# Three stages on one core: the first MoE's order written out by hand, and the second gate taken by 32-column blocks

## The chip, the cores and the metric

The kernel runs on one core of a Trainium2 chip. The metric is the device time of one execution in microseconds; 1963.57 is the median of three runs of the kernel before, which gave 1962.87 to 1965.89. TensorE is called PE, VectorE DVE, ScalarE ACT, GpSimd POOL, and SyncE, which issues most transfers, SP.

## The reference

Linear attention over 4 x 768 tokens gives x of 3072 tokens by 384. A first mixture of experts sends each token to one of 8 experts; a second one uses all 8 and weights them by a matrix P that is normalised by rows and columns in turn:

```python
# first MoE, top 1
e_idx = np.argmax(x @ w_gate, axis=1)
for e in range(E):
    mask = e_idx == e
    h = np.maximum(x[mask] @ w1[e], 0.0)
    out[mask] = gate_w[mask, None] * eom[mask, e, None] * (h @ w2[e])
...
# second MoE, all experts
logits = x @ w_gate
P = np.exp(logits - logits.max())
for _ in range(8):
    P /= P.sum(1, keepdims=True) + 1e-09
    P /= P.sum(0, keepdims=True) + 1e-09
    P *= N / E
for e in range(E):
    out += P[:, e:e + 1] * (np.maximum(x @ w1[e], 0.0) @ w2[e])
```

The arithmetic is float32. The kernel gets it from fp32r matmuls by splitting each operand into a high part (a cast) and a low part (the difference), with three matmuls for a product: high by high, high by low, low by high.

## The kernel before, in words

**Stage A** (0 to some 180 us) is the attention and the first gate. It leaves the tokens sorted by expert in device memory (`xs`), and 24 scatters on POOL (`tokd`, L785) still run when stage B begins.

**Stage B**, the first MoE, is a loop over 64 units `u` (8 experts by 8 slices of 128 hidden columns). `m_load` (L925) brings an expert's tokens in four transfers of 104 x 384 into one buffer `xe`, `m_tr` (L935) turns them with 12 PE transposes and splits them into `xh` and `xl`. A unit has nine matmuls of the first layer (`m_l1`, L958, into one of two PSUM buffers `l`), a split ReLU (`split_relu`: ACT L806 writes `hhm`, DVE L807 `hlm`), and, two units later, nine matmuls of the second layer (`m_l2`, L971). The weights of a unit come in one transfer on SP into one of three buffers `raw` (`w_load`, L99) and are split into `slot` by ACT (L112) and DVE (L113) in `w_conv`, six units ahead of their use at the start. At the end of an expert its three results are copied into `x2` (L976).

Work for stage C is put between the units in the program: `w_sums(0)` (sums of the second MoE's weights, POOL L832 to L837, from the transfers `ra` L817 and `rb` L822), `w_split(0, 0..2)` (their splits `wah` on ACT L850 and `wal` on DVE L851), called at units 58 to 60, and by the table `EARLY` sums of blocks of `x2` (`x_sum`, L890 and L891, on the engine that the table names, G for POOL, V for DVE) and their splits (`x_split`, ACT L900, DVE L901). Stage B is written in this order, but a scheduler may move each instruction within its engine's queue; each engine then runs its queue strictly in order. A branch (`If`, L1011) follows for tokens that overflow; it isn't taken here.

**Stage C**, the second MoE, has 32 units, each of 15 "products" of three fp32r matmuls with 512 columns (`product`, L1129) into the PSUM banks S, T, Z and W in the order of the table `ORDER`; `reads` adds or copies a bank into `hc` (ACT L1139, DVE L1142 to L1148) before the next product may use that bank. From unit 2 on the second layer's matmuls (`triple`, L1176) stand between the products. Here PE, DVE and ACT keep the order of the program (`manual_schedule`); POOL and SP are still the scheduler's. In unit 0 the remaining sums and splits of `x2` follow the table `FIRST`.

The second gate (`p_logits`, L1070) has for each of 24 token blocks of 128 three matmuls: the tokens are the stationary operand, the 8 gate columns (`wg2_raw`) move. Three are issued after each product of unit 0, four after those of unit 1. Each float32 matmul shows as two records in the trace. `p_max0` to `p_max2` (L1076 to L1090) take the maximum over all logits, subtract it and take the exponential into `pw`, in unit 1 at steps 7, 9 and 11. `sinkhorn` works on `pw` from unit 2 on.

Of the kernel before, what the change touches and what calls it, by code (L numbers as in the profile page):

```python
# [66 lines left out]
XBUF = [{"p11": 0, "p6": 1, "p3": 2, "p0": 2, "p5": 2, "p10": 2, "p1": 3, "p2": 4},  # L67
# [7 lines left out]
def linattn_moe_moe2_kernel(ctx: ExitStack, tc: tile.TileContext, a, out):  # L75
# [44 lines left out]
    maskb = const.tile([P, P], BF16, name="maskb")  # L120
# [29 lines left out]
    wg2_raw = const.tile([P, KD, E], F32, name="wg2_raw")  # L150
    nc.scalar.dma_start(wg2_raw, wg2)
# [745 lines left out]
    def x_split(hb, p):  # L897
# [7 lines left out]
             54: [("p5", V), "p9"], 55: ["p5"], 58: [("p10", V)], 62: ["p10"], 63: ["p6"], 64: ["p14"]}  # L905
# [13 lines left out]
    with ExitStack() as mctx:  # L919
# [57 lines left out]

        m_load(0)
        m_load(1)
        m_tr(0)  # L980
        NU = E * NF
        for u in range(NU + 2):
            if u < NU:
                if u + NWR < G5 + 5:
                    w_load(u + NWR)
                if u + NWR - 3 < G5 + 5:
                    w_conv(u + NWR - 3)
                if u + 2 >= G5 + 5:
                    w_conv(u + 2)
                if u + 5 >= G5 + 5:  # L990
                    w_load(u + 5)
                m_l1(u)
                if u == NU - 8:
                    r1_load(0)
                    r2_load(0)
                    w_sums(0)
                if u in (NU - 6, NU - 5, NU - 4):
                    w_split(0, u - NU + 6)
                if u == NU - 3:
                    r1_load(1)  # L1000
                if u % NF == 3:
                    m_load(u // NF + 2)
                if u % NF == 5:
                    m_tr(u // NF + 1)
            if u >= 2:
                m_l2(u - 2)
            for what in EARLY.get(u, ()):
                x_do(0, what)
# [65 lines left out]
    def p_max0():
        mxs["mx"] = m2.tile([P, 1], F32, name="pmx")
        V.tensor_reduce(mxs["mx"], mxs["lp"], AX.XY, ALU.max)  # L1076

    def p_max1():
        mp = qps.tile([P, P], F32, name="mxp", tag="o1")
        nc.tensor.transpose(mp[:1, :], mxs["mx"], ident)  # L1080
        mxs["m1"] = m2.tile([1, 1], F32, name="pm1")
# [165 lines left out]
    with tc.manual_schedule(engines={ENG.PE, ENG.DVE, ENG.Activation}):  # L1247
        for u in range(NU2):
# [4 lines left out]
            for s in range(15):  # L1253
# [99 lines left out]
```

## Time and profile before

| | |
|---|---|
| median of three runs | 1963.57 us (1962.87 to 1965.89) |
| the profiled execution, own time | 1965.2 us |
| its span, first to last instruction | 1963.4 us |
| mean granted clock of PE over the span | 0.971 |
| PE busy | 1901.3 us, 97% of the span |
| DVE, ACT, POOL busy | 1369.9, 832.9, 495.9 us (70%, 42%, 25%) |
| DMA | 123.49 MB, mean 63 GB/s |

The span is 1.8 us shorter than the time of the same execution: what lies before its first and after its last instruction. In the page's forty slices of 49 us PE is at nine tenths or more in all but five; the fifth (196 to 245 us), with the start of stage B, is at six. The granted clock is given as a share of full speed: 1.0 is 2.4 GHz, 0.5 is 1.2 GHz. A matmul's duration includes its way through the array, so what a row of several matmuls takes is the time from its start to the next row's start, not the sum of its records.

### The profile page before, as it was taken

The page shows a single profiled execution, that of the slowest core. Times are in us where ns is not written, and L with a number is a line of the kernel's source. Part 1 is how long each engine was busy: PE and PEld are TensorE (multiplying, and loading weights), DVE is VectorE, ACT ScalarE, POOL GpSimd, SP SyncE. Part 2 cuts the span into 40 slices and gives each one's busy share as a digit, 9 for nine tenths or more (in the row PEclk, how much of TensorE's full clock was granted, in tenths as well). Part 3 has the DMA queues.
Part 4 walks back from the last instruction along what each step waited for, and adds up shares of the span by engine and source line. Part 5 has one row for each costly group of instructions (what it writes and reads, how often), then busy time and mean ns, then how long its engine had stood idle before and what let it go on. Part 6 is the DMA issues. An engine that isn't in the chain of part 4 may idle for free.

```text
span 1963.4 us, 27510 instructions
## 1 busy us (share of the span) xinstructions
PE 1901.3 (97%) x10599; PEld 1723.3 (88%) x10600; DVE 1369.9 (70%) x2309; ACT 832.9 (42%) x1685; POOL 495.9 (25%) x528
## 2 busy tenths in 40 slices
PE   8988699999999999999999999999999999999998
PEld 6775699997889999999999988999999999999997
DVE  8995355564797767777667778667776777776774
ACT  4563344441545443444444344543444343434442
POOL 6786400112111121111111224311112211111112
PEclk8897899996999999999999999999999999999999
DMA  9864644210111111111111111111111111111101
GB/s 309 250 197 112 115 139 138 73 58 25 34 40 33 33 33 33 41 33 33 41 33 33 33 33 55 59 32 41 41 33 33 33 34 40 33 38 36 33 25 49
DMA packets 43987, 123.49 MB, mean 63 GB/s; under 512 B 6680, under 2 KB 10136, under 8 KB 43848
## 3 DMA queue, kind: packets, MB, share of 16 engines
q1 hardware_dynamic: 39256, 111.95, 19.5%
q0 software_dynamic: 3904, 9.47, 1.3%
q8 instruction: 85, 1.39, 0.3%
q14 instruction: 54, 0.44, 0.1%
q10 hardware_dynamic: 688, 0.23, 0.1%
HBM read 107.07 MB, written 14.56 MB: 62 GB/s over the span
## 4 chain that ended last, share of the span: by engine, by line
PE 74%; DVE 2%; issue 1%; POOL 0%; ACT 0%; POOLq 0%; DVEq 0%; ACTq 0%
PE o L1176 39%; PE bS L1129 13%; PE bT L1129 11%; PE bZ L1129 5%; PE bW L1129 4%; PE lgp L1070 1%; DVE wal L851 1%; DVE hc L1142 0%; DVE slot L901 0%; POOL out L1196 0%; DVE x L1194 0%; DVE hl L1163 0%; DVE third L901 0%; DVE xsb L890 0%; ACT slot L900 0%
## 5 line engine op out<-in xcount | busy, mean ns | idle before, releaser
L1176 PE MATMUL o<-wbh,hl 128*128 128x384 f32 x1536 | 515.1, 335 | 0.8 <-DVE hl L1163 0.7
L1176 PE MATMUL o<-wbh,hh 128*128 128x384 f32 x1536 | 514.2, 335 | 0.7 <-DVE x L1188 0.3
L1176 PE MATMUL o<-wbl,hh 128*128 128x384 f32 x1536 | 514.3, 335 | 0.0
L1163 DVE SCALAR_TENSOR_TENSOR hl<-hc,hh 128x512 fp32r<-128x512 f32 x384 | 275.2, 719 | 205.5 <-ACT hh L1162 201.6
L832 POOL TENSOR_TENSOR ws<-ra 128x384 f32<-128x384 f32 x64 | 64.9, 1014 | 1106.6 <-DVE wal L851 1023.7
L1176 PEld LDWEIGHTS o<-wbh,hh 128*128 128x128 f32 x1536 | 288.5, 188 | 46.7 <-DVE x L1194 1.1
L1176 PEld LDWEIGHTS o<-wbh,hl 128*128 128x128 f32 x1536 | 288.4, 188 | 42.4 <-DVE hl L1163 1.9
L1176 PEld LDWEIGHTS o<-wbl,hh 128*128 128x128 f32 x1536 | 288.5, 188 | 0.0
L1139 ACT COPY hc<-bT 128x512 f32<-128x512 f32 x192 | 112.7, 587 | 408.8 <-PE bT L1129 407.0
L1139 ACT COPY hc<-bS 128x512 f32<-128x512 f32 x192 | 112.5, 586 | 377.9 <-PE bS L1129 377.8
L1162 ACT ACTIVATE hh<-hc 128x512 fp32r<-128x512 f32 x384 | 240.2, 634 | 11.7 <-PE o L1176 10.3
L1129 PE MATMUL bS<-slot,wah 128*128 128x512 f32 x704 | 230.8, 402 | 8.7 <-DVE hc L1142 6.8
L1194 DVE SCALAR_TENSOR_TENSOR x<-o,pw,x 128x384 f32<-128x384 f32 x348 | 205.0, 611 | 22.4 <-PE o L1176 17.9
L1129 PE MATMUL bT<-slot,wah 128*128 128x512 f32 x640 | 205.0, 402 | 0.0
L1142 DVE TENSOR_TENSOR hc<-bS,hc 128x512 f32<-128x512 f32 x192 | 132.0, 688 | 47.0 <-PE bS L1129 45.7
L1129 PE MATMUL bS<-slot,wal 128*128 128x512 f32 x384 | 152.1, 396 | 0.0
L851 DVE TENSOR_TENSOR wal<-ws,wah 128x384 fp32r<-128x384 f32 (+2 forms) x192 | 132.6, 691 | 24.3 <-ACT wah L850 24.3
L1129 PEld LDWEIGHTS bS<-slot,wah 128*128 128x128 f32 x704 | 128.2, 190 | 11.0 <-DVE hc L1142 8.0
L1142 DVE TENSOR_TENSOR hc<-bT,hc 128x512 f32<-128x512 f32 x128 | 87.9, 687 | 56.6 <-PE bT L1129 53.7
L1129 PE MATMUL bT<-slot,wal 128*128 128x512 f32 x320 | 126.5, 395 | 0.0
L850 ACT CAST wah<-ws 128x384 fp32r<-128x384 f32 (+2 forms) x192 | 117.6, 613 | 13.7 <-POOL ws L837 13.7
L1129 PEld LDWEIGHTS bT<-slot,wah 128*128 128x128 f32 x640 | 115.7, 190 | 0.2
(227 smaller groups left out, 2915.2 us busy)
## 6 DMA issues: line engine op xcount, KB each, us to landing
raw<-in_wm SPq DMA_DIRECT2D x64, 384.0 KB
ra<-in_wm SPq DMA_DIRECT2D x64, 384.0 KB
rb<-in_wm SPq DMA_DIRECT2D x64, 384.0 KB
na<-in_nat SPq DMA_DIRECT2D x25, 576.0 KB
rk<-in_rkt SPq DMA_DIRECT2D x25, 448.0 KB
xs<-zer SPq DMA_DIRECT2D x8, 624.0 KB
xe<-xs SPq DMA_DIRECT2D x32, 156.0 KB
xs<-x,posl POOLq DMA_INDIRECT x24
```

Source lines behind the costliest of these rows:

```text
L832: G(s_[:, 0:3], r[:, 1], r[:, 0], ALU.subtract)
L850: nc.scalar.copy(hi[:, q], x)
L851: nc.vector.tensor_tensor(lo[:, q], x, hi[:, q].bitcast(F32), ALU.subtract)
L1070: nc.tensor.matmul(mxs["lp"][:, t, :], x2[:, k, t * P:(t + 1) * P], wg2_raw[:, k, :], start=(k == 0), stop=(k == KD - 1), skip_group_check ...
L1129: nc.tensor.matmul(bank[bk], w_[:, at, :], x_, start=(opens == 1 and n == 0), stop=(n == 2), skip_group_check=True)
L1139: A.copy(hid(u, *copy[p]), ps)
L1142: V.tensor_tensor(h, ps, h, ALU.add)
L1162: A.activation(hh, h, AF.Relu)
L1163: V.scalar_tensor_tensor(hl, h, 0.0, hh.bitcast(F32), ALU.max, ALU.subtract)
L1176: nc.tensor.matmul(ob[j], h_[:, j * P:(j + 1) * P], w_[:, c], start=(f == 0 and m == 0), stop=(f == 3 and m == 2))
L1194: V.scalar_tensor_tensor(acc, ob[j], wt, acc, ALU.mult, ALU.add)
```

## The change

Four things change.

1. Stage B's loop stands under `manual_schedule` for PE, DVE and ACT, so that these engines keep the program's order there too. `w_sums(1)` is now called in unit 63 of stage B, not in unit 0 of stage C.
2. The second gate has the gate's columns as the stationary operand, padded with zeros to 32 (`wg2_s`), and 512 tokens move. Blocks of tokens write PSUM partitions 0 to 31, 32 to 63 and so on: 18 matmuls of 32 x 512 in groups of four (steps 0 to 2 of unit 1) and of two (steps 3 to 5), where there were 72 of 128 x 8. ACT copies the sums to `xsb4` and `xsb3`; eight transposes (`p_turn`, steps 6 and 8 of unit 1) and two copies on DVE bring them into `pw`; the maximum follows at steps 8, 10 and 12.
3. `m_load` is one transfer of 624 KB where there were four of 156 KB.
4. The sum p1 of `x2` is taken on DVE in unit 64 of stage B, not on POOL in unit 0 of stage C, and the buffers of p1 and p2 are others.

```diff
-XBUF = [{"p11": 0, "p6": 1, "p3": 2, "p0": 2, "p5": 2, "p10": 2, "p1": 3, "p2": 4},
+XBUF = [{"p11": 0, "p6": 1, "p3": 2, "p0": 2, "p5": 2, "p10": 2, "p1": 2, "p2": 3},
...
-    wg2_raw = const.tile([P, KD, E], F32, name="wg2_raw")
-    nc.scalar.dma_start(wg2_raw, wg2)
+    wg2_s = const.tile([P, KD, 4 * E], F32, name="wg2_s")
+    nc.vector.memset(wg2_s[:, :, E:], 0.0)
+    nc.scalar.dma_start(wg2_s[:, :, 0:E], wg2)
...
-             54: [("p5", V), "p9"], 55: ["p5"], 58: [("p10", V)], 62: ["p10"], 63: ["p6"], 64: ["p14"]}
+             54: [("p5", V), "p9"], 55: ["p5"], 58: [("p10", V)], 62: ["p10"], 63: ["p6"], 64: ["p14", ("p1", V)]}
...
-            for j in range(CJ):
-                nc.sync.dma_start(t[:, j, :], xs[e * NTOK + j * CP:e * NTOK + (j + 1) * CP, :])
+            nc.sync.dma_start(t, xs[e * NTOK:e * NTOK + CAP, :].rearrange("(j p) d -> p j d", p=CP))
...
+        with tc.manual_schedule(engines={ENG.PE, ENG.DVE, ENG.Activation}):
...
+                    if u == NU - 1:
+                        w_sums(1)
...
-    def p_logits(n):
-        if "lp" not in mxs:
-            mxs["lp"] = qps.tile([P, NT, E], F32, name="lgp", tag="o0")
-        for _ in range(min(n, len(lgq))):
-            t, k = lgq.pop(0)
-            nc.tensor.matmul(mxs["lp"][:, t, :], x2[:, k, t * P:(t + 1) * P], wg2_raw[:, k, :], start=(k == 0),
-                             stop=(k == KD - 1), skip_group_check=True)
+    def p_logits(r, k):
+        nb = 4 if r == 0 else NB - 4
+        if k == 0:
+            mxs["l", r] = qps.tile([P, TB], F32, name=f"lgp{r}", tag=f"o{r}")
+        for q in range(nb):
+            n = 4 * r + q
+            nc.tensor.matmul(mxs["l", r][32 * q:32 * (q + 1), :], wg2_s[:, k, :], x2[:, k, n * TB:(n + 1) * TB],
+                             start=(k == 0), stop=(k == KD - 1), skip_group_check=True)
+        if k == KD - 1:
+            A.copy(xsb[4 - r][:32 * nb], mxs["l", r][:32 * nb])
+
+    def p_turn(r):
+        nb = 4 if r == 0 else NB - 4
+        tp = qps.tile([P, TJ, nb, 4 * E], F32, name=f"lgt{r}", tag=f"o{2 + r}")
+        for j in range(TJ):
+            nc.tensor.transpose(tp[:, j].rearrange("p q e -> p (q e)"), xsb[4 - r][:32 * nb, j * P:(j + 1) * P],
+                                ident[:32 * nb, :32 * nb])
+        V.tensor_copy(pw[:, 16 * r:16 * r + 4 * nb, :].rearrange("p (q j) e -> p j q e", j=TJ), tp[:, :, :, 0:E])
...
-        V.tensor_reduce(mxs["mx"], mxs["lp"], AX.XY, ALU.max)
+        V.tensor_reduce(mxs["mx"], pw, AX.XY, ALU.max)
...
-    FIRST = {0: ["p11", ("p1", G)], 1: ["p7"], 3: ["p12"], 4: [("p2", V)], 6: ["p1"], 7: ["p2"], 9: ["p4"]}
+    FIRST = {0: ["p11"], 1: ["p7"], 3: ["p12"], 4: [("p2", V)], 6: ["p1"], 7: ["p2"], 9: ["p4"]}
+
+    GATE = {15: [lambda: p_logits(0, 0)], 16: [lambda: p_logits(0, 1)], 17: [lambda: p_logits(0, 2)],
+            18: [lambda: p_logits(1, 0)], 19: [lambda: p_logits(1, 1)], 20: [lambda: p_logits(1, 2)],
+            21: [lambda: p_turn(0)], 23: [lambda: p_turn(1), p_max0], 25: [p_max1], 27: [p_max2]}
...
-                if u == 0:
-                    p_logits(3)
-                elif u == 1:
-                    p_logits(4)
-                    if s == 7:
-                        p_max0()
-                    if s == 9:
-                        p_max1()
-                    if s == 11:
-                        p_max2()
+                for step in GATE.get(15 * u + s, ()):
+                    step()
...
                 if s == 4:
-                    w_sums(u + 1)
+                    if u > 0:
+                        w_sums(u + 1)
```

Where instructions move: ACT's queue in the first five units of stage B, before:

```order
L112 CAST slot0_63<-raw9_2997 128x768
L806 ACTIVATE hhm3_3071<-l1_3_3061 128x416
L850 CAST wah0_0_4805<-ra0_4738 128x256
L112 CAST slot1_64<-raw10_3013 128x768
L850 CAST wah0_0_4805<-ws0_4742 128x384
L850 CAST wah0_1_4841<-ws0_4742 128x512
L850 CAST wah0_1_4841<-ra0_4738 128x128
L806 ACTIVATE hhm4_3103<-l1_4_3093 128x416
```

and the same place now (the lines are those of the changed kernel, one or more further down):

```order
L112 CAST slot0_63<-raw9_2994 128x768
L807 ACTIVATE hhm3_3068<-l1_3_3058 128x416
L112 CAST slot1_64<-raw10_3010 128x768
L807 ACTIVATE hhm4_3097<-l1_4_3087 128x416
L112 CAST slot2_65<-raw11_3026 128x768
L807 ACTIVATE hhm5_3124<-l1_5_3114 128x416
```

The casts of `wah0_*`, which read `ra0` and POOL's sums `ws0`, are no longer between the ReLUs of units 3 and 5. They stand at units 58 to 60, in the place where the program calls them; DVE's `wal0_*` go with them.

PE's queue at the start of stage C, before (each matmul of the gate counted once):

```order
L1129 MATMUL bS0_0_5179<-slot5_68,wah0_0_4805 128x512 x2
L1129 MATMUL bS0_0_5179<-slot5_68,wal0_0_4806 128x512
L1070 MATMUL lgp_5185<-wg2_raw_104,x2_2945 128x8 x3
L1129 MATMUL bT0_1_5191<-slot5_68,wah0_0_4805 128x512
L1129 MATMUL bT0_1_5191<-slot6_69,wah0_0_4805 128x512
L1129 MATMUL bT0_1_5191<-slot5_68,wal0_0_4806 128x512
```

and now, from the first step of unit 1, where the gate begins:

```order
L1143 MATMUL bS1_0_5270<-slot5_68,wah1_0_5227 128x512 x2
L1143 MATMUL bS1_0_5270<-slot5_68,wal1_0_5228 128x512
L1074 MATMUL lgp0_5276<-x2_2946,wg2_s_103 32x512 x4
L1143 MATMUL bT1_1_5281<-slot5_68,wah1_0_5227 128x512
L1143 MATMUL bT1_1_5281<-slot6_69,wah1_0_5227 128x512
L1143 MATMUL bT1_1_5281<-slot5_68,wal1_0_5228 128x512
L1074 MATMUL lgp0_5276<-x2_2946,wg2_s_103 32x512 x4
```

Unit 0's products follow one another with no gate between them, and unit 1 has a group after each of its first six.

POOL's queue behind the branch, before (`xsb` with a new number each time is another buffer; `ws` are the sums for unit 2's weights):

```order
L890 TENSOR_TENSOR xsb_5168<-x_2945 128x512
L890 TENSOR_TENSOR xsb_2956<-x_2945 128x512
L891 TENSOR_TENSOR xsb_5168<-xsb_5168,x_2945 128x512
L891 TENSOR_TENSOR xsb_2956<-xsb_2956,x_2945 128x512
L890 TENSOR_TENSOR xsb_2955<-x_2945 128x512
L891 TENSOR_TENSOR xsb_2955<-xsb_2955,x_2945 128x512
L890 TENSOR_TENSOR xsb_5168<-x_2945,xsb_2956 128x512
L891 TENSOR_TENSOR xsb_5168<-xsb_5168,xsb_2955 128x512
L890 TENSOR_TENSOR xsb_5169<-x_2945 128x512
L891 TENSOR_TENSOR xsb_5169<-xsb_5169,x_2945 128x512
L832 TENSOR_TENSOR ws_5383<-ra_5310 128x384
```

and now:

```order
L891 TENSOR_TENSOR xsb_2957<-x_2946 128x512
L892 TENSOR_TENSOR xsb_2957<-xsb_2957,x_2946 128x512
L891 TENSOR_TENSOR xsb_2956<-x_2946 128x512
L892 TENSOR_TENSOR xsb_2956<-xsb_2956,x_2946 128x512
L833 TENSOR_TENSOR ws_5318<-ra_5255 128x384
L834 TENSOR_TENSOR ws_5318<-ra_5255 128x512
L836 TENSOR_TENSOR ws_5318<-ra_5255 128x256
L837 TENSOR_TENSOR ws_5318<-ws_5318,ra_5255 128x128
L838 TENSOR_TENSOR ws_5318<-ws_5318,ra_5255 128x256
L891 TENSOR_TENSOR xsb_5159<-x_2946 128x512
L892 TENSOR_TENSOR xsb_5159<-xsb_5159,x_2946 128x512
L891 TENSOR_TENSOR xsb_5158<-x_2946,xsb_2957 128x512
```

Four of the ten sums stay at the branch. The last four, of which three show here and which write the buffers that now also hold the gate's sums, come after the sums of unit 2's weights and wait for `p_turn`. The five sums of unit 1's weights stand ahead of the branch, in POOL's queue after the sums of unit 50.

## Rows read from the trace of the kernel before

**Rows 1.** Windows: length, busy (instructions) of PE, PEld, DVE, ACT, POOL, clock, DMA share, GB/s

```profile
209.90:224.70 14.80, 0.00 (x0) 0.00 (x0) 1.78 (x5) 2.32 (x6) 9.69 (x11) 0.64 0.30 27
224.70:227.90 3.20, 3.19 (x10) 3.06 (x11) 3.20 (x7) 3.03 (x6) 1.48 (x1) 0.52 0.75 31
434.30:449.60 15.30, 15.21 (x99) 13.65 (x99) 14.02 (x13) 7.70 (x15) 13.52 (x9) 1.00 0.08 25
453.20:487.20 34.00, 33.98 (x119) 30.14 (x120) 7.89 (x13) 4.99 (x9) 4.05 (x5) 0.50 0.08 23
```

**Rows 2.** Waits, 180 to 260 us: waiter, releaser, total us, times, longest

```profile
PE l L958 <- DVE hlm L807: 15.4, 2, 14.8
ACT wah L850 <- POOL ws L837: 13.5, 1, 13.5
```

**Rows 3.** Timeline, 192 to 228 us: start, us, work, [idle before <-releaser]

```profile
192.89 0.70 SPq L817 DMA_DIRECT2D ra<-in_wm  x1
199.83 10.44 SPq L99 DMA_DIRECT2D raw<-in_wm  x2
201.85 1.28 PE L958 MATMUL l<-xh,slot 128*128 128x416 f32 x6
203.54 0.35 PE L971 MATMUL y<-hhm,slot 128*128 128x416 f32 x1
206.92 1.23 PE L942 MATMUL xp<-ident,xe 104*128 104x104 f32 x12
207.78 0.41 ACT L850 CAST wah<-ra 128x256 fp32r<-128x256 f32 x1 [6.89 <-DMA ra<-in_wm]
224.71 2.45 PE L958 MATMUL l<-xh,slot 128*128 128x416 f32 x6 [14.85 <-DVE hlm L807]
227.89 0.35 PE L971 MATMUL y<-hhm,slot 128*128 128x416 f32 x1
```

**Rows 4.** Timeline of stage B's first 10 us, PE

```profile
187.26 0.78 PE L942 MATMUL xp<-ident,xe 104*128 104x104 f32 x3 [0.92 <-DMA xe<-xs]
188.41 2.10 PE L958 MATMUL l<-xh,slot 128*128 128x416 f32 x5 [0.37 <-issue]
```

**Rows 5.** Timeline, PE, starts of units 0, 1 and 2 of stage C

```profile
434.34 0.74 PE L1129 MATMUL bS<-slot,wah 128*128 128x512 f32 x2 [0.88 <-ACTq L1011]
...
453.22 1.22 PE L1129 MATMUL bS<-slot,wah 128*128 128x512 f32 x2 [3.68 <-DVE hc L1142]
...
463.49 1.20 PE L1129 MATMUL bS<-slot,wah 128*128 128x512 f32 x2
...
493.70 0.73 PE L1129 MATMUL bS<-slot,wah 128*128 128x512 f32 x2 [1.09 <-ACT hc L1139]
```

**Rows 6.** Chain of waits, 434 to 500 us: start, us, what

```profile
454.87 1.08 PE lgp L1070 x6
455.95 1.48 PE bT L1129 x3
468.10 1.51 PE lgp L1070 x8
496.29 0.70 PE bT L1129 x3
```

**Rows 7.** Timeline, DVE, unit 0 of stage C and one row of unit 1

```profile
439.48 1.77 DVE L890 TENSOR_TENSOR xsb<-x 128x512 f32<-128x512 f32 x1
442.87 0.68 DVE L1142 TENSOR_TENSOR hc<-bT,hc 128x512 f32<-128x512 f32 x1
445.45 1.66 DVE L860 TENSOR_TENSOR wbl<-rb,wbh 128x768 fp32r<-128x768 f32 x1
483.68 0.95 DVE L860 TENSOR_TENSOR wbl<-rb,wbh 128x768 fp32r<-128x768 f32 x1
```

**Rows 8.** Timeline, PE, the first gate's 32-column blocks in stage A

```profile
100.46 0.42 PE L377 MATMUL sp<-xth,wg_s 128*32 128x128 f32 x6
100.81 0.67 PE L326 MATMUL sp<-na,kn 128*64 128x48 f32 x16
```

More of the change, by code (lines that the diff above doesn't have):

```diff
@@ L119, in linattn_moe_moe2_kernel @@
     ident = const.tile([P, P], F32, name="ident")
-    maskb = const.tile([P, P], BF16, name="maskb")
     onesf = const.tile([P, P], F32, name="onesf")
@@ L167, in linattn_moe_moe2_kernel @@
         mask = acst.tile([P, P], F32, name="mask")
+        maskb = acst.tile([P, P], BF16, name="maskb")
         nc.gpsimd.affine_select(out=mask, in_=onesf, compare_op=ALU.is_gt, fill=0.0, base=0,
@@ L976, in m_l2 @@
                     cp(x2[:, k, ds(offr[e], CAP)], yps[e][k])
[L978 to L1008, printed above, removed]
+        with tc.manual_schedule(engines={ENG.PE, ENG.DVE, ENG.Activation}):
+            m_load(0)
+            m_load(1)
+            m_tr(0)
+            NU = E * NF
+            for u in range(NU + 2):
+                if u < NU:
+                    if u + NWR < G5 + 5:
+                        w_load(u + NWR)
+                    if u + NWR - 3 < G5 + 5:
+                        w_conv(u + NWR - 3)
+                    if u + 2 >= G5 + 5:
+                        w_conv(u + 2)
+                    if u + 5 >= G5 + 5:
+                        w_load(u + 5)
+                    m_l1(u)
+                    if u == NU - 8:
+                        r1_load(0)
+                        r2_load(0)
+                        w_sums(0)
+                    if u in (NU - 6, NU - 5, NU - 4):
+                        w_split(0, u - NU + 6)
+                    if u == NU - 3:
+                        r1_load(1)
+                    if u == NU - 1:
+                        w_sums(1)
+                    if u % NF == 3:
+                        m_load(u // NF + 2)
+                    if u % NF == 5:
+                        m_tr(u // NF + 1)
+                if u >= 2:
+                    m_l2(u - 2)
+                for what in EARLY.get(u, ()):
+                    x_do(0, what)
@@ L1060, in linattn_moe_moe2_kernel @@
     third += [m2.tile([P, TB], F32R, name=f"third{q}") for q in range(3)]
-    lgq = [(t, k) for t in range(NT) for k in range(KD)]
     mxs = {}
-    def p_logits(n):
-        if "lp" not in mxs:
-            mxs["lp"] = qps.tile([P, NT, E], F32, name="lgp", tag="o0")
-        for _ in range(min(n, len(lgq))):
-            t, k = lgq.pop(0)
-            nc.tensor.matmul(mxs["lp"][:, t, :], x2[:, k, t * P:(t + 1) * P], wg2_raw[:, k, :], start=(k == 0),
-                             stop=(k == KD - 1), skip_group_check=True)
+    def p_logits(r, k):
[15 more added lines that the diff above has]
+        V.tensor_copy(pw[:, 16 * r:16 * r + 4 * nb, :].rearrange("p (q j) e -> p j q e", j=TJ), tp[:, :, :, 0:E])
     def p_max0():
         mxs["mx"] = m2.tile([P, 1], F32, name="pmx")
-        V.tensor_reduce(mxs["mx"], mxs["lp"], AX.XY, ALU.max)
+        V.tensor_reduce(mxs["mx"], pw, AX.XY, ALU.max)
     def p_max1():
-        mp = qps.tile([P, P], F32, name="mxp", tag="o1")
+        mp = qps.tile([P, P], F32, name="mxp", tag="o0")
         nc.tensor.transpose(mp[:1, :], mxs["mx"], ident)
@@ L1084, in p_max2 @@
     def p_max2():
-        mb = qps.tile([P, 1], F32, name="mxb", tag="o2")
+        mb = qps.tile([P, 1], F32, name="mxb", tag="o1")
         nc.tensor.matmul(mb, onesf[:1, :], mxs["m1"], start=True, stop=True)
@@ L1088, in p_max2 @@
         V.tensor_copy(nmx, mb)
-        V.tensor_scalar(pw, mxs["lp"], nmx, None, ALU.subtract)
+        V.tensor_scalar(pw, pw, nmx, None, ALU.subtract)
         A.activation(pw, pw, AF.Exp)
```

## The prediction

> **What bounds the kernel now.** I began with the page: PE is busy 97% of the span, so time can come only from stretches where PE idles, runs at the lower clock, or does work that falls away. The windows view, asked by stretches of stages B and C, shows where these are [rows 1]. From 209.9 to 224.7 us PE does nothing for 14.8 us; in the next 3.2 us it works at a clock of 0.52; from 453.2 to 487.2 us it is busy throughout, but at 0.50. From 487 us on PE is the bound at full clock, and the change leaves that alone.
>
> The list of waits names the hole's cause: PE waits 14.8 us for DVE's `hlm`, and ACT waits 13.5 us for POOL's sums `ws` [rows 2]. The timeline gives the order: ACT waited 6.89 us for the transfer `ra`, cast the first part of `wah`, and then stood at the next cast until POOL had made the sums, with the ReLU of unit 4 behind it in its queue [rows 3]. POOL was late because its scatters came first.
>
> In stage C the first product starts at 434.34, unit 1 at 463.49 and unit 2 at 493.70 us [rows 5]: 59.4 us for 30 products. At full clock a product takes 0.70 us, at half 1.48; the gate's share of a step is 1.08 (six records) or 1.51 us (eight) at half [rows 6]. In the first window of stage C, at full clock, 11 steps take 15.2 us of PE [rows 1], so a step's gate is 15.2 / 11 − 0.70 = 0.68 us. The clock fell behind an idle 3.68 us of PE before 453.22 [rows 5] and stayed down as long as the 8-column matmuls stood between the products.
>
> **Part 1, stage B by hand.** The casts of `wah` go to units 58 to 60, the ReLUs of units 3 to 5 stand behind nothing but weight casts, and the wait of 14.85 us has no cause left. With it goes the low clock behind it: nine matmuls of L958 took 227.89 − 224.71 = 3.18 us where they take 203.54 − 201.85 = 1.69 [rows 3], so 1.49 us. Together 16.3 us.
>
> What is late next is the weights. The transfer `raw12` is issued at 199.83 [rows 3], behind the split of unit 9 in both versions. `ra`, issued at 192.89, kept ACT waiting to 207.78, thus 14.9 us [rows 3]; at that price raw12 would land at 214.7. Units last 3.4 us (188.41 to 201.85 is four of them) [rows 3, 4], so its cast is due in unit 6, near 210 with the 12 transposes of 1.23 us. ACT then waits up to 4.7 us, and unit 6's ReLU with it; PE needs that only two units later, some 6 us. raw13 and raw14 follow in the same queue. Cost: 0 if the slack holds, 6 us if three transfers in turn are each some 2 us beyond it; I take 0.5, since only the first of them is issued into the same crowd. The work that covers it is one to two units of matmuls.
>
> `wah0` and `wal0` (1,920 columns) cost ACT and DVE some 3 us each, at the 0.41 us of one 256-column cast [rows 3], in the 10 us of units 58 to 60; both idle in a part of every unit, and what they deliver is used two units later: 0. p1's sum on DVE in unit 64 replaces POOL's and hides beside the second layer: 0. `w_sums(1)` on POOL lies ahead of the branch, beside the last units: 0; it would delay POOL's sums at the branch if the transfer came late.
>
> **Part 3, one load per expert.** At the start PE turned each 104-token piece as it came, the last at 187.26, and unit 0 began at 188.41 [rows 4]. In one piece, all 12 transposes come after the landing. If that is at the last piece's time, they end 1.23 us later [rows 3], about 0.3 behind before, or 1.7 at half clock; if SP's fewer issues land it sooner, −1. I take 0.3. Later experts are loaded two ahead: 0. **Stage B: 16.3 − 0.5 − 0.3 = 15.5, between 8.6 and 17.3.**
>
> **Part 2, unit 0.** Without 15 gates of 0.68 us PE wants 10.5 us for the 15 products, and DVE becomes the bound, since a bank is opened again only after DVE's add. Before, DVE reached p5's add (step 4) at 442.87 because its sums took 1.77 us beside POOL, where the same kind of work takes less alone: `wbl` is 1.66 beside POOL and 0.95 later [rows 7]. POOL was busy 13.5 of the first 15.3 us [rows 1]. Nine instructions took that, 1.5 us each; now it has four at the branch, some 6 us. So DVE is as slow as before to about 440.7 and then at its normal pace. p5's add is done at 442.7 to 443.5 and PE waits some 3 us before step 7; p11's add, with `wbl`, one split and half of unit 1's `wal` at uncontended length ahead of it, ends near 449.9, and PE waits another 2 to 3 us before step 11. The last four products: 449.9 + 4 x 0.70 = 452.7. Unit 1 starts at 452.7 to 455, say 453.5, not 463.49.
>
> **Part 2, unit 1.** Fifteen products: 10.5 us. The gate's groups: the first gate's three 32-column blocks side by side pass 6 records of 128 columns in 100.81 − 100.46 = 0.35 us [rows 8]; a group's 512 columns at this rate are 1.4 us. The 104-column transposes, 12 in 1.23 us [rows 3], give 0.5 us a record of 512, 1.0 for the two records of a matmul, if blocks overlap wholly. I take 1.2, the middle: 6 x 1.2 = 7.2. The transposes of the logits: 2 x 0.6 = 1.2, four at 0.10 and a wait for a copy. POOL's last four sums now fall into unit 1 and slow DVE as before in unit 0: a wait of 3 us before step 11. A row with one operand in PSUM took 0.68 us beside POOL [rows 7], so the adds themselves are not slowed; I count only splits. The clock falls behind the waits of unit 0, as it did at 453.22, but now 0.70 us products and 512-column groups follow; behind the hole of stage B such a stream ran 3.2 us at half clock and was then at 1.00 [rows 1, 3]. Twice that: 3.5 us. The exponential at the end: 1.5, like the 1.09 us wait of now [rows 5]. Sum 10.5 + 7.2 + 1.2 + 3 + 3.5 + 1.5 = 26.9; unit 2 starts at 480.4, say 481, not 493.70: 12.7. A short stretch at low clock behind the wait for the exponential takes 1.5 off. **Stage C: 11.2, between 2 and 17.**
>
> *A rule to weigh here.* The Trainium skill, page "SBUF — State Buffer", section "Who interferes with whom", says that of a DVE and a GpSimd instruction contending for the shared ports the second fully blocks, and that a DVE instruction with at most one SBUF input doesn't contend. The trace agrees on the second half (0.68 us). By the first half the four moved sums could block DVE for their whole length, 4 x 1.5 us, and the forecast would be some 3 us later.
>
> Sum: 15.5 + 11.2 = 26.7. The profiled execution would go from 1965.2 to 1938.5 us (span 1963.4 to 1936.7). The median of the runs is 1.6 us below that execution: 1963.57 − 26.7 = 1936.9, so **1937 us**.
>
> **The rivals.**
> - *The hole becomes a wait for transfers.* raw12 to raw14 land late one after the other, ACT's cast stands ahead of the ReLU, and 9 of the 16.3 us stay. For it: DMA engines were 14.9 us late with `ra`. Against: in the hole their share was only 0.30 [rows 1], so the queue had run dry. 1937 + 9 = 1946.
> - *Stage C gains all.* The clock doesn't fall (3.5 + 1.5) and POOL is out of DVE's way (1 in unit 0): 1937 − 6 = 1931. Against: POOL's sums are still in both units.
> - *The clock stays low through the gate groups,* as it did with the 8-column gates: six products at +0.78 and six groups at +1.2 are 11.9, of which 3.5 is counted and some lies in DVE's waits: +9 is 1946. For it: 34 us at 0.50 though PE was always busy [rows 1].
> - *Slower: the blocks of 32 columns run one after another.* Each matmul then takes 1.0 us, 18 of them 18 at full clock and 36 at half; with a quarter of the array at work the clock, low since unit 0's waits, stays down as with the 8-column gates. From 453.5 unit 1 needs 15 x 1.48 + 36 + 2.4 = 60.6, and unit 2 starts at 514.1: 20.4 later, less 15.5 in stage B: 1968.5. It decides when the groups take over 5 us on average. Against it stand the three blocks side by side [rows 8], six records in 0.35 us where one after another, at the transposes' rate (1.23 / 12 x 128 / 104), they would need 0.76. At full clock the serial blocks alone would be 1937 + 11 = 1948. Beside that row: the Trainium skill, "TensorE: Matmul & The Clock Gate", section "Measured speedup vs the span model", gives 2.38 times for three blocks of 32 columns with 512 moving; the trace's 0.76 to 0.35 is 2.2.
> - *The change doesn't do what it says* can be left out: the queues of ACT and PE are as written.
>
> **How the numbers follow.** A measurement of this kernel can tell about 0.2%, 4 us, from no change. Forecast 0.62 (1932 to 1943 by its own bounds), hole to transfers 0.12, all of it 0.12, low clock 0.10, slower or nothing 0.04. The range takes the forecast and the three next: 1928 to 1949. Faster needs a time under 1959.6; every case but the last has it, less 0.01 for what I haven't named: 0.95; same 0.02, slower 0.03.
>
> **What would show it.** In stage B PE's longest wait between 190 and 260 us should be under 3 us, no cast of `wah` should stand before unit 58, and first products should start near 419. Unit 0 should take 19 us with PE waiting twice for `hc`, unit 1 some 27, with groups of 1.0 to 1.4 us at full clock; unit 2 should start near 466. I am wrong if ACT waits for `raw` with PE behind it, if a group takes over 2 us at full clock, if the clock stays at 0.5 through unit 1, or if the rest after unit 2's start is longer than the 1469.3 us of now (1963.0 − 493.7).

## The result, and the profile after

The changed kernel took 1940.5 us in the median of four runs (1938.0 to 1941.7), the kernel before 1963.2 beside it: ratio 0.9881, 95% interval 0.9864 to 0.9899, some 23 us less. The forecast was 1937, the range 1928 to 1949. The profiled execution took 1938.0 us, its span is 1935.8: 27.6 less than that of before, some 5 more than the medians differ (stage A below).

I cut both profiles at the same five marks of the timeline: the first transfer of an expert's tokens (`xe`), the first matmul of stage B, and the first product of units 0, 1 and 2 of stage C.

| us | before | after | difference | forecast |
|---|---|---|---|---|
| stage A, to the first `xe` | 180.90 | 173.64 | −7.3 | 0 |
| to the first matmul of stage B | 7.51 | 8.80 | +1.3 | +0.3 |
| stage B to stage C | 245.93 | 239.14 | −6.8 | −15.8 |
| unit 0 | 29.15 | 17.93 | −11.2 | −10 |
| unit 1 | 30.21 | 23.80 | −6.4 | −2.7 |
| the rest | 1469.70 | 1472.49 | +2.8 | +1.5 |

The sum came out nearly right from terms that were wrong, and that is luck: stage B gave 9 us less than forecast, units 0 and 1 5 us more. Without stage A, whose 7 us aren't the change's as the experiments show, the differences add up to −20.3 where −26.7 was forecast.

The windows view of the profile after, with the columns of [rows 1], shows what is left:

```profile
182.40:209.90 27.50, 27.46 (x138) 26.76 (x138) 9.59 (x15) 7.74 (x14) 14.63 (x15) 0.91 0.95 121
209.90:212.40 2.50, 0.00 (x0) 0.00 (x0) 1.48 (x3) 2.21 (x4) 0.97 (x1) 1.00 1.12 96
222.40:226.30 3.90, 0.03 (x1) 0.00 (x0) 1.20 (x2) 2.06 (x5) 0.55 (x1) 0.85 0.50 194
226.30:232.00 5.70, 5.66 (x16) 5.40 (x17) 3.63 (x6) 2.49 (x4) 0.93 (x1) 0.50 0.74 169
430.00:433.50 3.50, 3.50 (x9) 2.78 (x10) 3.46 (x6) 1.82 (x4) 0.00 (x0) 0.52 0.00 0
439.50:450.90 11.40, 11.40 (x56) 3.89 (x55) 3.25 (x5) 2.87 (x5) 3.35 (x5) 1.00 0.11 36
```

The hole of 14.8 us is gone, but two holes of 2.5 and 3.9 us have taken its place, the second with 5.7 us at a clock of 0.50 behind it. In stage C the clock is low for 3.5 us, not 34, and it is 1.00 through all six groups of the gate (439.5 to 450.9).

The list of waits of the same profile, 180 to 260 us, names the new holes; against [rows 2] no wait for `ws` or `ra` is left:

```profile
ACT slot L112 <- DMA raw<-in_wm: 17.8, 3, 7.6
POOL tokd L786 <- DMA tokd<-tokid,cpi: 11.2, 8, 2.9
PE xp L942 <- DMA xe<-xs: 5.0, 1, 5.0
PE y L971 <- ACT x L976: 3.9, 1, 3.9
PE l L958 <- DVE hlm L808: 2.5, 1, 2.5
```

The timeline shows the order of it (rows of PE, SP, ACT and PE again; the first is the start of the stage):

```profile
179.75 2.31 PE L942 MATMUL xp<-ident,xe 104*128 104x104 f32 x12 [5.01 <-DMA xe<-xs]
...
193.56 7.10 SPq L99 DMA_DIRECT2D raw<-in_wm  x3
...
211.90 26.63 SPq L99 DMA_DIRECT2D raw<-in_wm  x8
...
210.06 0.83 ACT L112 CAST slot<-raw 128x768 fp32r<-128x768 f32 x1 [7.46 <-DMA raw<-in_wm]
...
224.24 0.83 ACT L112 CAST slot<-raw 128x768 fp32r<-128x768 f32 x1 [7.58 <-DMA raw<-in_wm]
...
212.43 1.40 PE L958 MATMUL l<-xh,slot 128*128 128x416 f32 x6 [2.54 <-DVE hlm L808]
...
226.34 0.71 PE L971 MATMUL y<-hhm,slot 128*128 128x416 f32 x1 [3.91 <-ACT x L976]
```

`raw12`, the weights of unit 12, issued at 193.56, was there at 210.06: 16.5 us. ACT stood at its cast, the ReLU behind it in the queue. The second long wait, of 7.58 us, was for the transfer issued at 211.90; behind it stood the ReLU and the copies of the first expert's result, which free the banks that PE wanted.

Stage C on PE, beside [rows 5]:

```profile
421.58 0.74 PE L1143 MATMUL bS<-slot,wah 128*128 128x512 f32 x2 [0.88 <-ACTq L1014]
...
429.99 1.22 PE L1143 MATMUL bT<-slot,wah 128*128 128x512 f32 x2 [3.27 <-DVE hc L1156]
...
436.05 0.74 PE L1143 MATMUL bS<-slot,wah 128*128 128x512 f32 x2 [1.49 <-DVE hc L1156]
...
440.41 1.06 PE L1074 MATMUL lgp<-x,wg_s 128*32 128x512 f32 x8
...
446.09 1.05 PE L1074 MATMUL lgp<-x,wg_s 128*32 128x512 f32 x4
...
458.07 0.73 PE L1143 MATMUL bS<-slot,wah 128*128 128x512 f32 x2 [2.12 <-DVE hc L1156]
...
463.31 0.72 PE L1143 MATMUL bS<-slot,wah 128*128 128x512 f32 x2 [1.67 <-ACT hc L1153]
```

Both waits of unit 0 stand before the steps that were named (7 and 11), of 3.27 and 1.49 us. The chain of waits has the price of a group and of a product beside one:

```profile
440.48 1.00 PE lgp L1074 x8
441.48 0.90 PE bT L1143 x3
...
446.16 0.98 PE lgp L1074 x4
```

A group of two blocks costs as much as one of four, and a product beside a group 0.90 us where it costs 0.70 alone.

### The profile page after: what moved, and what is told of

The parts are those of the page before. It is cut to its first block, busy times and chain, and to the rows that moved or that the text cites. A ratio compares the mean times of both kernels' runs of the same rounds, so it can differ in the third digit from the quotient of the medians.

```text
span 1935.8 us, 27273 instructions
## 1 busy us (share of the span) xinstructions
PE 1876.2 (97%) x10494; PEld 1699.7 (88%) x10500; DVE 1365.7 (71%) x2314; ACT 832.8 (43%) x1687; POOL 493.9 (26%) x526
## 4 chain that ended last, share of the span: by engine, by line
PE 75%; DVE 2%; issue 1%; ACT 0%; POOL 0%; POOLq 0%; DVEq 0%; ACTq 0%
PE o L1190 41%; PE bS L1143 14%; PE bT L1143 11%; PE bZ L1143 5%; PE bW L1143 4%; DVE wal L852 0%; DVE hc L1156 0%; PE lgp L1074 0%; POOL out L1210 0%; DVE slot L902 0%; DVE hl L1177 0%; ACT hc L1153 0%; DVE x L1208 0%; DVE third L902 0%; DVE wbl L861 0%
## 5 line engine op out<-in xcount | busy, mean ns | idle before, releaser
L1190 PEld LDWEIGHTS o<-wbh,hh 128*128 128x128 f32 x1536 | 289.1, 188 | 42.7 <-DVE x L1208 1.1
L1143 PE MATMUL bS<-slot,wah 128*128 128x512 f32 x704 | 226.1, 395 | 8.9 <-DVE hc L1156 6.4
L971 PE MATMUL y<-hhm,slot 128*128 128x416 f32 x384 | 114.8, 353 | 3.9 <-ACT x L976 3.9
```

Of the source, the lines that this page charges most:

```text
L971: nc.tensor.matmul(yps[e][k], w_[:, D + k * P:D + (k + 1) * P], h_[:, :CAP], start=(f == 0 and n == 0), stop=(f == NF - 1 and n == 2))
L1143: nc.tensor.matmul(bank[bk], w_[:, at, :], x_, start=(opens == 1 and n == 0), stop=(n == 2), skip_group_check=True)
L1190: nc.tensor.matmul(ob[j], h_[:, j * P:(j + 1) * P], w_[:, c], start=(f == 0 and m == 0), stop=(f == 3 and m == 2))
```

## The experiments

All runs were timed in turns with the kernel before on the same chip (its median was 1961.6 to 1966.1 there); a ratio is to that. The marks are those of one profile of each kernel, and an execution can differ from its kernel's median: five of the profiles (changed, a0_again, a6, a7, a8) have the changed kernel's stage B, and in them it took 235.4 to 241.3 us.

| kernel | median us | ratio (95%) | first `xe` | to stage B | stage B | units 0 + 1 | rest |
|---|---|---|---|---|---|---|---|
| before | 1963.2 | 1 | 180.9 | 7.5 | 245.9 | 29.2 + 30.2 | 1469.7 |
| changed | 1940.5 | 0.9881 (0.9864 to 0.9899) | 173.6 | 8.8 | 239.1 | 17.9 + 23.8 | 1472.5 |
| a0_again | 1942.1 | 0.9890 (0.9874 to 0.9905) | 177.0 | 8.9 | 240.9 | 17.9 + 23.8 | 1471.5 |
| b1_order | 1956.9 | 0.9958 (0.9942 to 0.9974) | 178.4 | 9.2 | 233.4 | 29.2 + 30.2 | 1470.9 |
| b2_gate | 1954.8 | 0.9945 (0.9932 to 0.9959) | 178.6 | 9.3 | 247.4 | 18.8 + 23.9 | 1471.9 |
| a3_four_loads | 1944.0 | 0.9873 (0.9852 to 0.9894) | 180.1 | 6.2 | 243.8 | 17.9 + 24.5 | 1472.9 |
| a4_loads_late | 1941.4 | 0.9878 (0.9861 to 0.9895) | 179.3 | 8.9 | 232.2 | 17.9 + 24.1 | 1472.5 |
| a5_scatter_spread | 1928.5 | 0.9825 (0.9811 to 0.9839) | 175.5 | 8.8 | 229.7 | 17.9 + 23.8 | 1472.5 |
| a6_gate_unit0 | 1934.6 | 0.9851 (0.9837 to 0.9864) | 177.5 | 8.7 | 238.8 | 18.2 + 18.7 | 1471.8 |
| a7_serial_gate | 1952.3 | 0.9936 (0.9918 to 0.9955) | 179.7 | 9.3 | 235.4 | 18.0 + 34.0 | 1472.5 |
| a8_pool_late | 1940.1 | 0.9877 (0.9860 to 0.9893) | 176.7 | 8.7 | 241.3 | 16.6 + 22.0 | 1474.0 |
| c1_scatter_gate | 1927.8 | 0.9810 (0.9795 to 0.9826) | 180.0 | 9.0 | 228.7 | 18.2 + 19.1 | 1472.3 |
| c2_four_loads | 1925.4 | 0.9805 (0.9787 to 0.9823) | 177.9 | 6.5 | 228.8 | 18.2 + 19.1 | 1472.2 |
| c3_pool_late | 1924.3 | 0.9795 (0.9777 to 0.9813) | 179.4 | 8.7 | 229.8 | 16.9 + 14.7 | 1473.3 |

**The parts alone.** b1_order is the kernel before with stage B under `manual_schedule` and `w_sums(1)` in it; b2_gate is the kernel before with the new gate alone.

> The kernel before with part 1 alone (stage B in program order, the sums for unit 1 called there). Theory: the 14.85 us hole and the 1.5 us at half clock behind it go, and what came back in the changed kernel (PE waits of 2.5 and 3.9 us whose cause is late weight transfers, and some 2.6 us at half clock) comes back here too: first product to the first ReLU unit gains 7 us of 245.9, stage C stays at 59.4 us from unit 0 to unit 2, 1956 us. Rival: the late transfers belong to the single load per expert, and with four loads all of 16 us is gained: 1947.

> The kernel before with part 2 alone (the gate's columns stationary, in unit 1). Theory: stage C from unit 0 to unit 2 takes 42 to 45 us where it took 59.4, PE's hole in stage B stays at 14 to 15 us, 1947. Rival: with ten POOL sums still at the branch DVE holds unit 0 back as before (PE waits of some 7 us in unit 0), and stage C takes 48 or more: 1952.

The ratios are 0.9958 and 0.9945, together 1.0% or 19 us, where the whole change gives 1.1 to 1.2%. b1 came out as its theory says by the time (1956.9), and the four loads didn't keep the weights from being late (ACT waited 20.1 us for them, PE 3.4 for ACT and DVE); but its stage B took 233.4, not 239. b2's theory held by its marks, 42.7 us for units 0 and 1 and a hole of 14.6, and missed by the time: 11 us less, not 16.6. Its profile lost 1.8 us before stage B, 1.5 in it and 2.3 in the rest against that of before; why stays open. b1's units 0 and 1 are those of before, and the windows of its profile say why they are long, with the 8-column matmuls in them:

```profile
438.00:455.00 17.00, 15.12 (x53) 13.39 (x54) 5.38 (x9) 1.39 (x3) 0.34 (x1) 0.50 0.08 24
455.00:475.00 20.00, 20.00 (x70) 17.48 (x71) 5.47 (x10) 3.62 (x7) 4.06 (x5) 0.50 0.06 20
```

The rival for b2_gate counted ten POOL sums at the branch; there were six, since the last four wait for the gate's buffers there too. Unit 0 took 18.8 us, 0.9 more than with four. Part 4 has no run of its own; this is about what it can be worth in unit 0.

**The same kernel again.** a0_again has no edit.

> The changed kernel as it is, on the same chip as the next three. Theory: stage A's end varies from run to run (first load of an expert's tokens at 173.6 us in the changed kernel's profile, 178.4 to 180.9 in four others) and is no effect of the change: here it lies at 177 to 181, and stage B is shorter than 239 us by about as much, since the weights land by the clock of the transfers, not of PE. Rival: the change ends stage A earlier: again near 173.6. Ratio to before 0.987 to 0.990.

The theory on stage A held: 177.0, and over all fourteen profiles 173.6 to 180.9, with no order by kernel (b1 and b2, whose stage A is that of before, have 178.4 and 178.6). The 7.3 us of the table above are mostly those two executions'. Its second half fell: stage B was no shorter with the later start (240.9). In both profiles ACT waits 17.8 and 20.6 us for weights.

**What the weights wait for.** First the two transfers `ra` and `rb`, put off to unit 56:

```diff
-            nc.sync.dma_start(r1[u].rearrange("p a k c -> p (a k c)"), wm2[u // NQ % E, u % NQ, 0])
+            op = nc.sync.dma_start(r1[u].rearrange("p a k c -> p (a k c)"), wm2[u // NQ % E, u % NQ, 0])
+            if u == 0:
+                tc.keep_in_program_order(op)
...
-            nc.sync.dma_start(r2[u], wm2[u // NQ % E, u % NQ, 1])
+            op = nc.sync.dma_start(r2[u], wm2[u // NQ % E, u % NQ, 1])
+            if u == 0:
+                tc.keep_in_program_order(op)
```

> The changed kernel with the two transfers for unit 0 of stage C issued by SP in the program's place (unit 56), not ahead of the weights of unit 12. Theory: 768 KB less stand ahead of those weights in the queue, ACT's waits for them fall from 17.8 us to under 8 and PE's from 6.5 to under 2, with 2 to 3 us less at half clock: 1932 to 1936. Rival: the weights wait for POOL's scatters of single words, not for these two transfers: PE's waits stay within 2 us of the changed kernel's, 1940.

ACT still waited 15.3 us, and the time is the changed kernel's (0.9878): the expected gain didn't come. The profile by itself leans the other way, with 2.3 us of waits on PE and 232.2 for stage B, where the five profiles with the changed kernel's stage B have 4.2 to 8.9 and 235.4 to 241.3; but it is of the fastest of four executions (1937.2, the others 1940.6 to 1942.5). A small part for these two transfers isn't excluded. Then POOL's scatters:

```diff
-        for i in range(NT):
+        def scatter(i):
+            nc.vector.tensor_copy(cpi[:, i:i + 1], cpi[:, i:i + 1])
...
+                if 16 <= u < 16 + NT:
+                    scatter(u - 16)
```

> The changed kernel with POOL's 24 scatters of single words spread over units 16 to 39 of stage B, one a unit behind a copy of its column on DVE. Theory: the weights of units 12 to 15 wait behind these scatters; without them ACT's waits for weights fall from 15 to 18 us to under 5, PE waits under 1 us in stage B, and the stage takes 226 to 229 us from its first matmul to stage C: some 5 us less than the changed kernel on this chip. Rival: the transfers of tokens and weights themselves fill the queues: ACT's waits stay over 10 us and the time within 2 us of the changed kernel's.

0.9825, 13.6 us below a0_again, where some 5 were expected; some 11 of them are in stage B (229.7, just over the expected 229). The scatters were the cause: ACT has no wait for `raw` in the list, PE none over 0.4 us within the stage, and stage B's window is all work:

```profile
184.30:414.00 229.70, 228.81 (x1236) 225.70 (x1237) 125.29 (x198) 102.98 (x172) 41.29 (x39) 0.99 0.55 116
```

The three later profiles with the scatters spread have 228.7 to 229.8 as well. The windows of 20 us that begin some 16.4 us behind the first `xe`, of the changed kernel and of a5_scatter_spread, show the DMA engines (the last two columns are their busy share and GB/s):

```profile
190.00:210.00 20.00, 19.90 (x112) 19.42 (x111) 6.83 (x10) 5.90 (x10) 9.87 (x10) 1.00 0.94 116
192.00:212.00 20.00, 20.00 (x114) 19.88 (x114) 10.47 (x14) 9.05 (x15) 4.84 (x5) 1.00 0.48 134
```

With the scatters the engines are busy twice as long and move less. In which queue or engine they hold the weights up, no run shows. The view of the scatters' line has their landing times, when they come at once (changed kernel) and one a unit (a5_scatter_spread):

```profile
L786 POOL DMA_INDIRECT tokd<-tokid,cpi x24: 963/967/1168, 173.4 to 214.0; - x24
...
DMA to landing us min/median/max: 6.7/15.0/16.9
```

```profile
L788 POOL DMA_INDIRECT tokd<-tokid,cpi x24: 962/966/984, 243.6 to 325.2; - x24
...
DMA to landing us min/median/max: 2.8/5.5/8.0
```

**One load per expert.** a3_four_loads and c2_four_loads undo part 3, in the changed kernel and in c1_scatter_gate.

> The changed kernel with the four loads per expert of before. Theory: part 3 is worth little: unit 0 of stage B starts within 1.5 us of the changed kernel's distance behind its first load, the waits for weights stay, 1940 to 1942. Rival: the single load is what made stage B start earlier and the weights late: the distance from the first load to the first unit is 1 to 2 us shorter, ACT's waits for weights fall from 17.8 us to under 10, 1936.

> The kernel of c1_scatter_gate with four loads per expert again. Theory: the transposes start as the pieces land, unit 0 begins 1 to 2.5 us earlier behind the first load (6.2 us in a3_four_loads, 8.7 to 8.9 with one load), and SP's further issues hide: 1 to 2.5 us less. Rival: 7.5 to 9.3 us, as in the other three profiles with four loads: the same time within 1 us.

Unit 0 of stage B starts 6.2 and 6.5 us behind the first load, with one load 8.7 to 9.3: against these two, part 3 costs 2.4 to 2.6 us there, so a3's theory was wrong in this and its rival nearer (ACT's waits fell to 11.9 us). The time doesn't show it: c2's median is 2.4 us under c1's, but the intervals overlap, and in a3 stage B took 243.8 us, with a wait of PE for DVE of 5.0. That four loads took 7.5 to 9.3 in before, b1_order and b2_gate is left open, so this cost is not shown for four loads in general.

**The gate's blocks.** a7_serial_gate gives each block PSUM partitions 0 to 31 of its own bank, so all use the same 32 columns:

```diff
-            mxs["l", r] = qps.tile([P, TB], F32, name=f"lgp{r}", tag=f"o{r}")
+            mxs["l", r] = [qps.tile([4 * E, TB], F32, name=f"lgp{r}_{q}", tag=f"o{q}") for q in range(nb)]
...
-            nc.tensor.matmul(mxs["l", r][32 * q:32 * (q + 1), :], wg2_s[:, k, :], x2[:, k, n * TB:(n + 1) * TB],
+            nc.tensor.matmul(mxs["l", r][q], wg2_s[:, k, :], x2[:, k, n * TB:(n + 1) * TB],
```

> The changed kernel with every block of 512 tokens written to PSUM partitions 0 to 31 of a bank of its own, so that all matmuls of the gate use the same 32 columns of the array; ACT makes four and two copies of 32 partitions where there was one each. Theory: the blocks then run one after another, 0.46 us a record: groups of four take 3.7 us and groups of two 1.9 at full clock, unit 1 takes 10 to 12 us longer than 23.8, the time 1952. Rival: the array takes them no faster side by side than in turn, and unit 1 stays within 2 us.

As expected: 1952.3, unit 1 at 34.0. The timeline has a group of four and one of two, the windows view the clock over all six:

```profile
443.18 3.62 PE L1074 MATMUL lgp<-x,wg_s 128*32 128x512 f32 x8
446.73 0.74 PE L1144 MATMUL bT<-slot,wah 128*128 128x512 f32 x2
...
456.51 1.90 PE L1074 MATMUL lgp<-x,wg_s 128*32 128x512 f32 x4
```

```profile
442.29:464.00 21.71, 21.71 (x56) 6.56 (x56) 3.22 (x5) 5.33 (x10) 4.07 (x5) 1.00 0.06 19
```

3.55 us to the next product for four blocks in turn, 1.00 side by side. The clock stayed at 1.00 here too.

**The gate in the waits of unit 0.** a6_gate_unit0 moves the groups to where PE waits:

```diff
...
-    GATE = {15: [lambda: p_logits(0, 0)], 16: [lambda: p_logits(0, 1)], 17: [lambda: p_logits(0, 2)],
-            18: [lambda: p_logits(1, 0)], 19: [lambda: p_logits(1, 1)], 20: [lambda: p_logits(1, 2)],
-            21: [lambda: p_turn(0)], 23: [lambda: p_turn(1), p_max0], 25: [p_max1], 27: [p_max2]}
+    GATE = {6: [lambda: p_logits(0, 0), lambda: p_logits(0, 1), lambda: p_logits(0, 2)],
+            10: [lambda: p_logits(1, 0), lambda: p_logits(1, 1), lambda: p_logits(1, 2)],
+            8: [lambda: p_copy(0)], 12: [lambda: p_copy(1)],
+            16: [lambda: p_turn(0)], 18: [lambda: p_turn(1), p_max0], 20: [p_max1], 22: [p_max2]}
```

> The changed kernel with the gate's groups in unit 0, where PE waits for DVE (three behind step 6, three behind step 10), the copies at steps 8 and 12, the transposes and the maximum early in unit 1. Theory: 4.8 us of waits take up six groups of 1.0 us, and the clock doesn't fall there: units 0 and 1 together take 36 to 38 us, not 41.7, 4 to 6 us less in all. Rival: DVE's chain sets unit 1 as well, since POOL's last four sums come earlier: together 40 or more.

36.9 us for both units, 4.8 less, as expected; unit 0 took all six groups for 0.25 us. The median is 7.6 us under a0_again's, 2.8 more than these marks explain. Here the groups follow one another, and the price of a record can be read: 24 records of four blocks in the time of 12 of two, 2.78 / 6 = 0.46 us for 512 columns whatever stands beside them.

```profile
430.09 2.78 PE L1074 MATMUL lgp<-x,wg_s 128*32 128x512 f32 x24
...
437.07 2.77 PE L1074 MATMUL lgp<-x,wg_s 128*32 128x512 f32 x12
```

**POOL out of DVE's way.** a8_pool_late and c3_pool_late pin POOL's sums for the second half of the tokens to units 13 to 15 (`keep_in_program_order` in `x_sum`).

> The changed kernel with POOL's sums for the second half of the tokens kept at their place in the program (units 13 to 15 of stage C), not behind the branch and in unit 1. Theory: DVE's rows with two operands in SBUF take 0.7 to 0.95 us in units 0 and 1 where they took up to 1.8, PE's waits for DVE there fall from 7.1 us to under 3, units 0 and 1 take 36 to 38 us. Rival: what is won there is lost at units 13 to 15, where the same sums then meet DVE: the rest behind unit 2 grows from 1472.5 by 3 us or more, and the time is the same.

> The scatters spread and the gate in unit 0 together. Theory: the two gains lie in different stages and add up: against the changed kernel 13.6 + 7.6 = 21 us, ratio to before 0.978 to 0.980, 1921. Rival: with stage C earlier, POOL or a transfer is late at the branch and takes 3 us or more back: 1924 or more.

> The kernel of c1_scatter_gate with POOL's sums for the second half of the tokens at units 13 to 15. Theory: with the gate in unit 0 the waits for DVE there are mostly filled (2.5 us of waits are left in unit 0 and 2.9 in unit 1), so little is to be had; units 0 and 1 gain 2 to 3 us and the rest loses 1.5 to 2.5: within 1.5 us of c1_scatter_gate. Rival: 3 us or more less.

In a8 units 0 and 1 gained 3.1 us, the rest lost 2.5, and the time is within the interval of a0_again: mostly the rival. What POOL's sums do to DVE is in the rows of both engines in unit 1 of the changed kernel:

```profile
452.32 1.29 POOL L891 TENSOR_TENSOR xsb<-x 128x512 f32<-128x512 f32 x1 [0.68 <-PE lgt L1083]
452.64 1.78 DVE L861 TENSOR_TENSOR wbl<-rb,wbh 128x768 fp32r<-128x768 f32 x1
...
455.55 1.59 POOL L891 TENSOR_TENSOR xsb<-x,xsb 128x512 f32<-128x512 f32 x1
455.93 1.49 DVE L852 TENSOR_TENSOR wal<-ra,wah 128x256 fp32r<-128x256 f32 x1
```

Without POOL's sums beside them such a `wbl` takes 0.95 us [rows 7] and this `wal` 0.42 (unit 1 of c3). Here `wbl` ended 0.81 us after the POOL instruction in which it began had ended (453.61), and `wal` 0.28 us after its own (457.14): each did almost all of its work when that instruction was over.

c1_scatter_gate has both gains by its marks (stage B 228.7, units 37.2). Its ratio is 0.9810 where the ratios of the two apart add up to 0.9786, so by the time its rival came true. But the marks of the two apart add up to 11.1 + 4.8 = 15.9 us, and c1 is 0.0080, some 15.7 us, under a0_again: nothing needs to have been taken back, and the 21 us were built on medians that differ by more than the marks.

In c3 I was wrong: units 0 and 1 fell from 37.2 to 31.6 us, the rest lost 1.0, and the median is 3.5 us under c1's, though the intervals overlap. The reason is POOL's queue more than the length of DVE's rows. In unit 1 of c1

```profile
445.25 1.26 POOL L893 TENSOR_TENSOR xsb<-x,xsb 128x512 f32<-128x512 f32 x1
446.47 0.72 POOL L840 TENSOR_TENSOR ws<-ws,ra 128x256 f32<-128x256 f32 x1
447.22 0.51 ACT L853 CAST wah<-ws 128x384 fp32r<-128x384 f32 x1 [1.85 <-POOL ws L840]
447.77 1.06 DVE L854 TENSOR_TENSOR wal<-ws,wah 128x384 fp32r<-128x384 f32 x1 [2.20 <-ACT wah L853]
449.82 1.22 PE L1149 MATMUL bS<-slot,wah 128*128 128x512 f32 x2 [4.41 <-DVE hc L1162]
```

the last sum of unit 2's weights (`ws`) stands behind three of the last four sums of `x2` in POOL's queue and is ready 11.3 us into the unit, in c3 8.7. ACT waits for it, DVE for ACT, and PE, at step 11, 4.41 us for DVE. The next five microseconds run at a clock of 0.51. In c3 those sums come in units 13 to 15, and the same step is

```profile
446.03 0.73 PE L1150 MATMUL bS<-slot,wah 128*128 128x512 f32 x2 [1.62 <-DVE hc L1163]
```

with the clock at 1.00 behind it. Of the 4.4 us by which unit 1 is shorter, 2.8 are the wait and 1.6 the steps behind it.

c3 has the lowest median of all runs: 1924.3 us, 0.9795 of before, some 16 to 18 us under the changed kernel. c2's four loads on top of it were not tried.

## Why the prediction was right, and where it was not

- **The hole of stage B** went as argued: no ReLU stands behind `wah` any more, and b1_order alone shows it.
- **The weights behind it: wrong.** I took 0.5 us, "since only the first of them is issued into the same crowd". Without late weights the stage takes 229.7 us (a5), the 245.9 − 16.3 of the working; with them 239.1, and 235.4 to 241.3 in all five profiles of that stage. So the term was 6 to 12 us, about its own bound of 6 at the least, and the rival with 9 us came true in size. What failed is that only the first meets the crowd: four transfers of weights were issued between 193.56 and 211.90, and the scatters from 173.4 to 214.0, so all four stood among them; that the scatters last so long stood in the trace of before (the first at 181.5, the last at 217.3). The DMA share of 0.30 in the hole was read as a queue that has room. It was the mean of a stretch in which SP issued one transfer, at 209.94, and no other up to 224.99, while ACT stood still. The old wait hid the next one. Stage B with its start gave 5.5 us, outside the 8.6 to 17.3 that I had allowed for it.
- **One load per expert:** +0.3 taken, +1.3 measured against before, within the bound of 1.7 at half clock, and that was the case: the 12 transposes took 2.31 us, not 1.23. The load itself was there 6.1 us behind its issue, where the last piece of before took 6.4, so the landing was taken rightly. In a3 and c2 the last piece was turned at 4.7 and 4.8 us, which makes the 2.4 to 2.6 against these; the working had only the trace of before.
- **Unit 0:** 17.9 us against 19.2, both waits in place. The low clock that I counted in unit 1 was here: the 3.5 us at 0.52, behind the first wait.
- **Unit 1:** 23.8 against 27.5. A group cost 1.0 us, not 1.2, and the product beside it 0.2 more, which cancels. What was over-sized is the clock: 3.5 us counted for unit 1 (twice the 1.49 us behind the hole is 3.0) and 1.5 behind the exponential, and in both stretches it was 1.00. The wait before step 11 was 2.12 (3 taken), the one for the exponential 1.67 (1.5).
- **The two rules.** The Trainium skill, "SBUF — State Buffer", section "Who interferes with whom", calls the shared port pair an exclusive lock; that the other engine fully blocks for the whole instruction it says of DVE's two-port modes, and of two SBUF inputs only that they contend with a GpSimd instruction that reads SBUF. The rows agree on who interferes (two operands in SBUF: 0.95 to 1.78; one in PSUM: 0.68 all along) and show the blocking for two SBUF inputs too: in unit 0 four such DVE rows ended 0.54 to 0.56 us after the POOL instruction in which they began, and alone they take 0.68; unit 1 is shown above. So the price is what is left of POOL's running instruction, 0.5 to 1.1 us a row here, not its whole 1.3 to 1.9. In unit 1 POOL's sums cost 1.8 us in the changed kernel (a8_pool_late against a0_again, 3 taken), and 4.4 once the gate is out of that unit (c3 against c1), mostly by POOL's queue. On the rival with the blocks in turn, a7 gives 3.55 us to 1.00: a factor of 3.5 for four blocks, so the forecast's side was right. The Trainium skill, "TensorE: Matmul & The Clock Gate", section "Measured speedup vs the span model", has 2.38 for three blocks, and no run here has three in turn.
- **The rest** was taken as unchanged but for 1.5 us of clock; it is 1.8 to 2.8 longer in the two profiles of the changed kernel. The others have 1.2 (b1_order) to 3.2 (a3_four_loads), a8_pool_late and c3_pool_late apart (4.3 and 3.6), which have POOL's late sums in it. The profile page's mean for a matmul of the second layer is 337 to 338 ns in every profile with the new gate, and 335 in before and b1_order; no wait in the lists explains it, and it stays open.
- **The signs.** Two of the four by which I would be wrong came: ACT waited for `raw` with PE behind it, and the rest was longer than before. (Its length before is 1469.7, the span being 1963.4; the 1469.3 of the prediction is a slip.) PE's longest wait in stage B was 3.9 us, not under 3. The other two didn't come.

## What to carry to other kernels

When a wait is taken away, ask what else ran while everything stood still: its transfers now meet those of the work that moved forward, and a low DMA share inside a stall may say only that nobody was issuing. Many small scatters can be cheap to issue (0.97 us of POOL each here) and dear for the loads beside them; if their result is needed late, spread them over a stage that leaves POOL free. Look also at what stands behind a moved instruction in its own queue: in c1 that cost more than the ports that two engines share. Work that only PE needs belongs where PE already waits for another engine.

## What the runs showed that I had not expected

- Records of 512 columns took 0.46 us with four blocks of 32 columns side by side, with two, and 0.45 with one (3.62 / 8); a 128-column product next to such a group took 0.90 us, not 0.70, also when the group's blocks ran in turn (a7).
- The clock stayed at 1.00 through 18 matmuls of 32 columns, in turn or side by side. Between the same products 8-column ones ran for 15.2 us at 1.00 at the start of unit 0 of before, and after an idle 3.68 us of PE for 34 us at 0.50; the same came in b1_order.
- A DVE instruction with both operands in SBUF that began within one of POOL's sums ended some 0.13 us less than its own length after that sum had ended, in six rows of units 0 and 1.
- 24 scatters of 128 words took a median of 15.0 us to land when issued together, and 5.5 when issued one every 3.5 us.
